# The last K load by partition quarters, a new order of TensorE's work at the end, and another way to the gate and the queries, in a one-token attention kernel

## The chip, the cores and the metric

The kernel runs on one core of a Trainium2 chip. The metric is the device time in microseconds (us). The span in a profile is some 2.1 us shorter than the measured time of the same run (before: 2523.2 against 2525.35). Repeated runs of one kernel lie within about 0.2%, so 5 us. In the lines of profiles below, PE is TensorE, DVE VectorE, ACT ScalarE and SP SyncE, and L324 is line 324 of that kernel.

## The reference

One token attends over a long cache, and a small gate network multiplies the result:

```python
B, Sq, D = 1, 1, 448;  H, Sk, Dh = 16, 65536, 256;  F = 1792
xn = layernorm(x)
q  = (xn @ wq).reshape(B, Sq, H, Dh).transpose(0, 2, 1, 3)
p  = softmax(einsum("bhqd,bhkd->bhqk", q, k_cache) * Dh ** -0.5)
o  = einsum("bhqk,bhkd->bhqd", p, v_cache)
s  = o.transpose(0, 2, 1, 3).reshape(B, Sq, H * Dh) @ wo
g  = silu(silu(xn @ w1) @ w2)
return x + s * g
```

K and V are bf16 and make 1.07 GB of the 1.084 GB that are read. No byte of them is used twice.

## The kernel before

The caches are read in 64 blocks each of 8 MB: 128 keys in each of the 128 partitions (rows) of SBUF, the memory on the chip that loads write to; 64 KB per partition. Three buffers of that size hold K or V in turn. VectorE and ScalarE make the scores of a K block, TensorE multiplies the exponentials with a V block, two keys per product. Semaphores free the buffers for the next load, which SyncE issues. (The code is cut and shortened; the comments are added.)

```python
def load_k(i, s):                      # a block of K over all 128 partitions
    take(sp, vf[s])
    sp.dma_start(out=R[s][:, :], in_=block(Kd, i)).then_inc(kl[s], 16)
...
def load_keys(T, src, k0, k1, s):      # keys k0 to k1 of every partition
    w = slice(k0 * Dh, k1 * Dh)
    sp.dma_start(out=T[:, w], in_=src[:, w]).then_inc(s, 16)
...
        take(sp, vf[0])                # after the loop: the last K, in two halves of 4 MB
        load_keys(R[0], Kl, 0, HK, kl[0])
        load_keys(R[0], Kl, HK, KB, kh[0])
        take(sp, kf[2])                # then V, in pieces
        ...
        # TensorE at the end (shortened)
        keys(psO2, 0, 1, vz, zl, 0, 2, True, od)
        pe_turn()                      # transposes one result row (line 346)
        project(...)                   # products with wo (line 662)
        ...
        keys(psO, 0, 1, vz, zl, 2, 3, True)
        pe_turn()
        keys(psO, 0, 1, vz, zl, 3, len(vz), False, od)
        act_out()
        project(*pieces[2])
        t = pe_turn(tok=True)
        ...
        project(pieces[3][0], H1); project(H1, H)   # last head, then result
```

The head of the kernel computes gate's first product as 112 products of one column each, and the 16 queries as 64 products 256 wide.

## Time and profile before

| | before |
|---|---|
| measured time | 2525.48 us, median of 3 (2525.09 to 2526.38) |
| span of the profile | 2523.2 us |
| bytes read | 1084.29 MB |
| mean rate of the DMA engines | 430 GB/s |
| VectorE busy | 2233.7 us, 89% |
| TensorE busy | 1198.1 us, 47% |

The page's line of GB/s has one figure for each of 40 equal slices, 63 us long:

```profile
GB/s 423 417 430 433 434 431 433 433 432 432 432 432 432 433 434 437 434 435 433 433 433 432 432 432 432 432 433 434 439 434 433 433 433 433 432 432 432 432 412 346
```

After the first slices the rate is flat at some 432, and only the last two, where small pieces of V and the end fall, are clearly lower. One stretch of 20 us in which the last K comes in (length, then busy us of TensorE, its weight loads, VectorE, ScalarE, GpSimd with the count of instructions, TensorE's granted clock, DMA share, GB/s):

```profile
2446.00:2466.00 20.00, 14.24 (x72) 6.28 (x69) 12.14 (x59) 10.45 (x51) 0.00 (x0) 0.90 0.98 418
```

### The profile page before, as it was taken

How to read it: one execution, taken by the hardware profiler on the slowest of the kernel's cores; microseconds unless marked ns; L12 is line 12 of the kernel's file. 1: busy time of each engine (PE TensorE's matmuls, PEld its weight loads, DVE VectorE, ACT ScalarE, POOL GpSimd, SP SyncE). 2: the span in 40 equal slices, each digit the busy share in tenths (PEclk: the TensorE clock that was granted, in tenths of full speed). 3: DMA queues.
4: the chain of work that ended last, by engine and by line, in shares of the span. 5: the costliest groups of instructions: out<-in, count | busy, mean ns of one | idle time of the engine just before them, and what ended most of it. 6: DMA issues, size and time to landing. Idle time of an engine off the chain costs nothing. (4 is left out here: it accounts for less than half of the span.)

```text
span 2523.2 us, 29918 instructions
## 1 busy us (share of the span) xinstructions
PE 1198.1 (47%) x5125; PEld 500.5 (20%) x5125; DVE 2233.7 (89%) x10281; ACT 1443.9 (57%) x6992; POOL 2.5 (0%) x13
## 2 busy tenths in 40 slices
PE   3353543534535435445354354454553543534556
PEld 2121211212212112112121121221221211212222
DVE  6989889889899898898898988988989889889886
ACT  3656556556555565565565655655656556556554
POOL 0000000000000000000000000000000000000000
PEclk7676767767767767677676676676766767767778
DMA  9999999999999999999999999999999999999998
GB/s 423 417 430 433 434 431 433 433 432 432 432 432 432 433 434 437 434 435 433 433 433 432 432 432 432 432 433 434 439 434 433 433 433 433 432 432 432 432 412 346
DMA packets 22728, 1084.52 MB, mean 430 GB/s; under 512 B 2354, under 2 KB 4532, under 8 KB 4916
## 3 DMA queue, kind: packets, MB, share of 16 engines
q1 hardware_dynamic: 22706, 1084.30, 99.5%
q8 instruction: 6, 0.10, 0.0%
q14 instruction: 14, 0.11, 0.0%
q10 hardware_dynamic: 2, 0.00, 0.0%
HBM read 1084.29 MB, written 0.00 MB: 430 GB/s over the span
## 5 line engine op out<-in xcount | busy, mean ns | idle before, releaser
L271 ACT ACTIVATE R<-R 128x256 bf16<-128x256 bf16 x3328 | 1330.7, 401 | 697.1 <-ACTq L154 697.1
L249 DVE CUSTOM_DVE_ANT_0 R<-R,qcur 128x256 bf16<-128x256 bf16 x4864 | 1700.2, 417 | 0.0
L318 PE MATMUL bank<-R,PV 128*2 128x512 bf16 x4096 | 1023.7, 416 | 32.4 <-DMA R<-in_A_v_cache_dram 15.3
L238 DVE TENSOR_TENSOR R<-R,qcur 128x3328 bf16<-128x3328 bf16 x256 | 482.6, 1885 | 198.7 <-DVEq L154 198.6
L271 ACT ACTIVATION_READ_ACCUMULATOR R<-R 128x1 f32 x3328 | 620.2, 186 | 2.6 <-issue 2.6
L330 PE MATMUL bank<-ident,rmax 128*1 128x128 bf16 x65 | 17.1, 263 | 1021.6 <-PEq L154 1021.6
L318 PEld LDWEIGHTS bank<-R,PV 128*2 128x2 bf16 x4096 | 365.0, 90 | 663.1 <-issue 208.0
L249 DVE DVE_READ_ACCUMULATOR2_ANT S<- 128x1 f32 x4864 | 383.5, 79 | 0.0
L346 PE MATMUL bank<-eye,O 2*128 2x1 f32 x536 | 98.0, 300 | 236.8 <-PEq L154 236.8
L330 PEld LDWEIGHTS bank<-ident,rmax 128*1 128x1 bf16 x65 | 5.2, 79 | 1026.1 <-issue 1025.9
L346 PEld LDWEIGHTS bank<-eye,O 2*128 2x128 f32 x536 | 94.2, 257 | 254.8 <-issue 254.8
L284 ACT ACTIVATE hist<-bank 128x1 f32 (+1 forms) x65 | 11.1, 171 | 203.4 <-ACTq L154 203.4
L305 ACT COPY hist<-bank 128x2 f32 (+1 forms) x66 | 10.5, 160 | 120.0 <-ACTq L154 120.0
L214 DVE TENSOR_REDUCE gmax<-bank 1x1 bf16<-1x128 f32 x65 | 18.2, 281 | 36.2 <-DVEq L154 36.2
L231 DVE CAST qcur<-bank 128x256 bf16<-128x256 f32 x64 | 27.2, 425 | 20.2 <-DVEq L154 18.3
L297 ACT COPY O<-bank 2x512 f32<-2x512 f32 x67 | 37.5, 559 | 9.1 <-ACTq L154 9.1
L286 ACT ACTIVATE PV<-S,hist 128x128 bf16<-128x128 f32 (+1 forms) x65 | 26.0, 400 | 13.4 <-ACTq L154 13.1
L358 PE MATMUL bank<-q,ident 16*128 16x256 bf16 x63 | 24.4, 387 | 0.0
L224 DVE COPY S<-S 128x128 f32<-128x128 f32 (+1 forms) x65 | 14.7, 226 | 9.5
L225 DVE TENSOR_REDUCE rmax<-S 128x1 bf16<-128x128 f32 (+1 forms) x65 | 18.2, 279 | 0.0
L336 PE MATMUL bank<-gmax,ones_row 1*128 1x1 bf16 x65 | 10.3, 158 | 15.9 <-PEq L154 15.9
L336 PEld LDWEIGHTS bank<-gmax,ones_row 1*128 1x128 bf16 x65 | 6.5, 99 | 33.3 <-issue 33.3
(65 smaller groups left out, 101.7 us busy)
## 6 DMA issues: line engine op xcount, KB each, us to landing
R<-in_A_k_cache_dram SPq DMA_DIRECT2D x4, 4096.0 KB, 23.4
R<-in_A_v_cache_dram SPq DMA_DIRECT2D x7, 2048.0 KB, 23.1
R<-in_A_wq_dram SPq DMA_DIRECT2D x1, 3072.0 KB, 12.7
R<-in_A_wo_dram SPq DMA_DIRECT2D x2, 1120.0 KB, 17.5
R<-in_B_w_dram SPq DMA_DIRECT2D x1, 1568.0 KB, 27.2
R<-in_B_w_dram SPq DMA_DIRECT2D x1, 1344.0 KB, 5.8
R<-in_A_v_cache_dram SPq DMA_DIRECT2D x1, 1024.0 KB, 15.8
R<-in_A_v_cache_dram SPq DMA_DIRECT2D x2, 512.0 KB, 17.0
```

Of the source, the lines that this page charges most:

```text
L214: dve.reduce_max(out=gmax[0:1, :], in_=ps_m[0:1, :], axis=AX.X).then_inc(gm, 1)
L225: dve.reduce_max(out=rmax[:, :], in_=S[:, c0:c1], axis=AX.X).then_inc(rm, 1)
L231: dve.tensor_copy(out=qcur[:, :], in_=ps_q).then_inc(sd, 1)
L238: m = dve.tensor_tensor(out=pair, in0=pair, in1=qcur[:, None, :].to_broadcast([P, NA, Dh]), op=ALU.mult,)
L249: ins = dve.tensor_tensor_reduce(out=Kv[:, c, :], in0=Kv[:, c, :], in1=qcur[:, :], scale=1.0, scalar=0.0, op0=ALU.mult, op1=ALU.add, accum ...
L271: ins = act.activation(out=prod, in_=prod, func=ACT.Identity, accum_out=S[:, c : c + 1],)
L286: act.activation(out=PV[s][:, c0:c1], in_=S2[:, c0:c1], func=ACT.Exp, bias=col(0, 1), scale=scale, accum_out=col(1, 2),).then_inc(pv, 1)
L297: act.copy(out=O[:, :], in_=po).then_inc(oc, 1)
L318: ins = pe.matmul(po, lhsT=PV[t][:, c : c + 2], rhs=R[s][:, c * Dh : (c + 2) * Dh], start=(start and c == k0), stop=(stop and c == k1 - 2),)
L330: pe.matmul(ps_m[0:1, :], lhsT=rmax[:, 0:1], rhs=ident[:, :], start=True, stop=True).then_inc(tm, 1)
L346: ins = pe.matmul(ps_t[:, a : a + 1], lhsT=Ov[:, j, a, :], rhs=eye2[:, j : j + 1], start=(j == 0), stop=(j == 1),)
L358: pe.matmul(ps_q, lhsT=ident[0:H, at(h)].to_broadcast([H, P]), rhs=q16[:, :], start=True, stop=True,).then_inc(qr, 1)
```

## The change

The change means to cut what lies at the ends of a stream that is full in between. It loads the last K in eight pieces by partition quarters, moves work of TensorE into its pauses while the last V arrives, computes gate's first product as a row (16 wide products) that is then transposed, and makes the queries of two heads in one product.

```diff
-    vz = cuts(0, 32, 64, 96, 112, 120, 128)
+    vz = cuts(0, 32, 64, 80, 96, 112, 120, 128)
-    pieces = cuts(0, 5, 10, 14, 16)
+    pieces = cuts(0, 5, 12, 14, 16)
+    kr = cuts(0, 32, 64, 96, 128)
...
-        load_keys(R[0], Kl, 0, HK, kl[0])
-        load_keys(R[0], Kl, HK, KB, kh[0])
+        for (c0, c1), sm in zip(cuts(0, HK, KB), (kl[0], kh[0])):
+            for p0, p1 in kr:
+                load_keys(R[0][p0:p1, :], Kl[p0:p1, :], c0, c1, sm)
...
-        for f in range(FC):               # gate: 112 products of one column
-            for z in range(2): ...
+        for g, b in enumerate((0, 1, 5, 6)):   # gate: 16 products of 1x448
+            ...
+            t = mark("act", act.copy(out=h1r[:, g * FQ : (g + 1) * FQ], in_=bank[b][0:1, 0:FQ]))
         for f in range(FC):
+            ins = pe.matmul(ps_h[:, f : f + 1], lhsT=h1r...[:, f, :], rhs=ones_sq[0:1, 0:1], ...)
...
-        for h in range(H):                # 64 products, 256 wide
+        for j in range(HP):               # 32 products, 512 wide
...
-        keys(psO2, 0, 1, vz, zl, 0, 2, True, od)
+        keys(psO2, 0, 1, vz, zl, 0, 1, True)
         pe_turn()
+        keys(psO2, 0, 1, vz, zl, 1, 2, False, od)
...
         project(h0 + 3, h1)
-        act_softmax(LAST + 1, 0, HK, KB)
+        pe_turn()
...
-        keys(psO, 0, 1, vz, zl, 2, 3, True)
-        pe_turn()
-        keys(psO, 0, 1, vz, zl, 3, len(vz), False, od)
+        keys(psO, 0, 1, vz, zl, 2, len(vz), True, od)
```

(Cut: the tiles and offsets that follow from these, VectorE's wait, which now counts all loads of a half, and where ScalarE's parts of the end are written down. Some comments are added and some lines shortened.)

More of the change, by code (lines that the diff above doesn't have):

```diff
@@ L60 @@
     NHA = H * 2
+    HP = H // 2
     scale = float(Dh) ** -0.5
@@ L74 @@
     qcur = pool.tile([P, Dh], bf16, name="qcur")
-    q16 = pool.tile([H, Dh], bf16, name="q16")
+    q8 = pool.tile([HP, 2 * Dh], bf16, name="q8")
     S = pool.tile([P, KB], fp32, name="S")
@@ L109 @@
     wq_t, n = rest(0, DF * HD + HD // 2)
-    Z, n = rest(n, DX * H * H)
+    Z, n = rest(n, DX * HP * HP)
     w1_t, n = rest(n, DF * F + F // 2)
@@ L114 @@
     xz, n = rest(n, 2 * P)
+    h1r, n = rest(n, 2 * F)
     assert n <= KW
+    h1r = h1r[0:1, :].bitcast(fp32)
     xn, xz = xn[0:1, :], xz[0:1, :].rearrange("o (z n) -> o z n", z=2)
@@ L127 @@
     ps_q, ps_y, ps_ao, ps_tot = bank[4][:, 0:Dh], bank[5][0:1, 0:D], bank[6][0:1, 0:D], bank[7]
-    psO2, ps_qh = bank[4][0:2, :], bank[3][0:H, 0:Dh]
+    psO2, ps_qh = bank[4][0:2, :], bank[3][0:HP, :]
     ps_xt, ps_h = bank[2][:, 0:DX], bank[7][:, 0:FC]
@@ L232, in dve_block @@
         halves = between is not None
-        take(dve, kl[s], 16)
+        n = 16 * len(kr) if halves else 16
+        take(dve, kl[s], n)
         for k in range(NSTEP):
             if k == NSTEP // 2:
-                take(dve, kh[s], 16)
+                take(dve, kh[s], n)
             pair = Kv[:, k * SUB + ND : (k + 1) * SUB, :]
@@ L356, in pe_query @@
     def pe_query(i):
-        h = i // NB
+        j = i // (2 * NB)
+        o = ((i // NB) % 2) * Dh
         pe.matmul(
             ps_q,
-            lhsT=ident[0:H, at(h)].to_broadcast([H, P]),
-            rhs=q16[:, :],
+            lhsT=ident[0:HP, at(j)].to_broadcast([HP, P]),
+            rhs=q8[:, o : o + Dh] if isinstance(o, int) else q8[:, bass.ds(o, Dh)],
             start=True,
@@ L489 @@
         for c in range(DX):
-            w = Z[:, c * H * H : (c + 1) * H * H]
+            w = Z[:, c * HP * HP : (c + 1) * HP * HP]
             t7 = mark("dve", dve.tensor_copy(
-                out=w[:, 0 : (H - 1) * (H + 1) + 1 : H + 1],
-                in_=xnT[:, c : c + 1].to_broadcast([P, H]),
+                out=w[:, 0 : (HP - 1) * (HP + 1) + 1 : HP + 1],
+                in_=xnT[:, c : c + 1].to_broadcast([P, HP]),
             ))
@@ L505 @@
         pe.wait_ge(dl["w1"], 32)
-        for f in range(FC):
-            for z in range(2):
-                h0 = z * (P // 2)
-                for r, (w, c) in enumerate(rows(w1_t, F, z * (F // 2), (z + 1) * (F // 2))):
-                    ins = pe.matmul(
-                        ps_h[h0 : h0 + P // 2, f : f + 1],
-                        lhsT=w.rearrange("p (q f) -> p f q", f=FC)[:, f, :],
-                        rhs=xnT[:, c : c + 1],
-                        start=(r == 0),
-                        stop=(r == DF),
-                    )
+        FQ = F // 4
+        for g, b in enumerate((0, 1, 5, 6)):
+            for r, (w, c) in enumerate(rows(w1_t, F, g * FQ, (g + 1) * FQ)):
+                ins = pe.matmul(
+                    bank[b][0:1, 0:FQ],
+                    lhsT=xnT[:, c : c + 1],
+                    rhs=w,
+                    start=(r == 0),
+                    stop=(r == DF),
+                )
+            t = mark("pe", ins)
+            need("act", t)
+            t = mark("act", act.copy(out=h1r[:, g * FQ : (g + 1) * FQ], in_=bank[b][0:1, 0:FQ]))
+        need("pe", t)
+        for f in range(FC):
+            ins = pe.matmul(
+                ps_h[:, f : f + 1],
+                lhsT=h1r.rearrange("o (p f) -> o f p", f=FC)[:, f, :],
+                rhs=ones_sq[0:1, 0:1],
+                start=True,
+                stop=True,
+            )
         t = mark("pe", ins)
@@ L543 @@
         ins.then_inc(qr, 1)
-        for h in range(H):
-            for r, (w, c) in enumerate(rows(wq_t, HD, h * Dh, (h + 1) * Dh)):
+        for j in range(HP):
+            for r, (w, c) in enumerate(rows(wq_t, HD, j * 2 * Dh, (j + 1) * 2 * Dh)):
                 ins = pe.matmul(
                     ps_qh,
-                    lhsT=Z[:, (c * H + h) * H : (c * H + h + 1) * H],
+                    lhsT=Z[:, (c * HP + j) * HP : (c * HP + j + 1) * HP],
                     rhs=w,
-                    start=(h == 0 and r == 0),
-                    stop=(h == H - 1 and r == DF),
+                    start=(j == 0 and r == 0),
+                    stop=(j == HP - 1 and r == DF),
                 )
@@ L554 @@
         need("act", t8)
-        t9 = mark("act", act.copy(out=q16[:, :], in_=ps_qh))
+        t9 = mark("act", act.copy(out=q8[:, :], in_=ps_qh))
         pe.wait_ge(dl["w2"], 16)
@@ L694 @@
         act_softmax(LAST, 0, 0, HK)
+        act_out()
         act_sums(0, 2)
-        act_out()
+        act_row(LAST - 1)
         act_sums(0, 3)
-        act_row(LAST - 1)
         take(pe, pv)
-        keys(psO2, 0, 1, vz, zl, 0, 2, True, od)
+        keys(psO2, 0, 1, vz, zl, 0, 1, True)
         pe_turn()
+        keys(psO2, 0, 1, vz, zl, 1, 2, False, od)
+        act_out(psO2)
+        act_softmax(LAST + 1, 0, HK, KB)
         need("pe", t_o)
@@ L717 @@
         weights(N1, NENT, H1, H, (ps_m[:, 0:NL], t15))
-        act_out(psO2)
-        keys(psO, 0, 1, vz, zl, 2, 3, True)
-        pe_turn()
+        t_r = mark("act", act_row(LAST))
         t_g = silu(g_t, ps_y, g_e, t_y)
-        t = mark("act", act_row(LAST))
-        need("dve", t)
+        need("dve", t_r)
         outputs(N1, NENT - 1, H1, H, NL - 1)
-        keys(psO, 0, 1, vz, zl, 3, len(vz), False, od)
+        keys(psO, 0, 1, vz, zl, 2, len(vz), True, od)
         act_out()
```

## The prediction

> **What bounds the kernel now.** I read the page first, then the chain that ended last, then the timelines of TensorE, VectorE and the DMA queue near the end, then busy time by stretches. On the page, lines of its head, slices and queues:
>
> ```profile
> span 2523.2 us, 29918 instructions
> ...
> DVE  6989889889899898898898988988989889889886
> ...
> DMA  9999999999999999999999999999999999999998
> ...
> HBM read 1084.29 MB, written 0.00 MB: 430 GB/s over the span
> ```
>
> The 16 DMA engines are full in every slice; VectorE, the busiest engine, never is. A full stretch moves some 432 GB/s, so the 1084 MB take 1084.3 / 0.432 = 2510 us. The other 13 us are a start, a few holes and what follows the last bytes. The change moves no byte more or fewer, so it can only win or lose in those 13 us, or by the rate of the stream. The chain of work that ended last (start us, us, what):
>
> ```profile
> 2484.34 23.09 DMA R<-in_A_v_cache_dram
> 2507.43 0.04 issue
> 2507.47 3.61 PE bank L318 x16
> 2511.08 1.03 PE bank L346 x8
> 2512.11 3.54 PE bank L318 x16
> 2515.66 1.51 PE bank L662 x8
> 2517.17 1.03 PE bank L346 x8
> 2518.20 0.95 PE bank L662 x4
> ```
>
> A piece of the last V (32 of 128 keys) lands at 2507.43, then TensorE works almost unbroken, then VectorE twice 0.6 us and the write of the result; the span ends at 2523.2. (The measured 2525.5 is 2.3 us over the span.) One more place matters, in TensorE's timeline and in the stretches of 4 us (busy us per engine, clock, DMA share, GB/s):
>
> ```profile
> 2420.18 1.44 PE L318 MATMUL bank<-R,PV 128*2 128x512 bf16 x3
> 2427.17 15.35 PE L318 MATMUL bank<-R,PV 128*2 128x512 bf16 x61 [5.55 <-issue]
> 2442.35 0.17 PE L368 MATMUL bank<-ident 128*1 128x1 bf16 x1
> ```
>
> ```profile
> 2436.00:2440.00 4.00, 4.00 (x21) 1.53 (x19) 4.00 (x25) 3.14 (x16) 0.00 (x0) 1.00 1.14 492
> 2440.00:2444.00 4.00, 3.17 (x19) 1.58 (x17) 4.00 (x14) 0.57 (x1) 0.00 (x0) 1.00 0.46 139
> ```
>
> TensorE stops 5.55 us for "issue", in the middle of a block's products, soon after it left its loop. The buffer for the last K is therefore free only at 2442.5, the queue issues that K at 2442.65, and the DMA engines have run dry: 139 GB/s, a hole of about 2.5 us. VectorE stops likewise on leaving its loop:
>
> ```profile
> 2458.56 0.28 DVE L214 TENSOR_REDUCE gmax<-bank 1x1 bf16<-1x128 f32 x1 [0.94 <-DVEq L154]
> 2465.61 0.42 DVE L231 CAST qcur<-bank 128x256 bf16<-128x256 f32 x1 [6.77 <-DVEq L154]
> ```
>
> Its query was ready at 2458.6 (TensorE's product of line 358 ran at 2458.34) and the first half of the last K had landed at 2454.7 (issued 2442.65, 12.0 us), so this is no wait for data.
>
> [...] The kernel before loads caches only over 128 partitions, at 432 GB/s[...]. [...] stretches with TensorE idle show 0.50, and its 128x512 products come every 0.43 us then, 0.22 us otherwise.
>
> **The change, part by part.**
>
> Gate's first product. Removed: 112 products (6.71 us at 7.45 to 14.16). Added: 16 products of 1x448, which I put at 0.2 to 0.3 us from the 0.2 us pitch of line 662 and 0.32 of line 561, so 3.2 to 5 us; four ScalarE copies of one row, some 0.55 us each from its 1x448 exponential of 0.53, three beside the products; 14 float32 transposes of two passes, 28 x 0.13 us (line 346: eight passes in 1.07) = 3.7 us. It ends near 16 to 17 us instead of 14.2. TensorE then waits for wq, which lands at 17.1, as before. VectorE enters its loop 2 to 3 us later and pays its entry pause there (before: idle 5.74 us up to 20.80), so has its query at 23 to 24; its first work on K started at 27.25, when that half landed. Hidden: 0 us.
>
> Queries of two heads. 64 products (8.79 us) become 32 twice as wide, some 7 us. The result is wanted by the second block, at 61.7 us, and w2's product waits for its DMA till 30.9. Hidden: 0 us. In the loop each query gains a register instruction; TensorE is idle about half the time: 0 us.
>
> TensorE's order at the end. One transpose (1.03 us, line 346) moves before the second V piece, into a 2.37 us wait for it; the transpose of the second half moves before the last products, so the chain holds one transpose instead of two. Four projection products, 4 x 0.2 us, move from after V to before it, with their 448 KB. From before's times: the maximum is broadcast at 2504.95, then 8 projections 1.6 = 2506.65, transpose 1.03 = 2507.7, sums 0.36 = 2508.05. The exponential, done at 2505.98, is in time, and the first V piece, now half as long, too. All 32 products in one go: 32 x 0.222 = 7.1, ending 2515.15 (before 2515.58). Their last piece lands later by 448 KB at the 390 GB/s of these stretches, 1.15 us: 2512.6 becomes 2513.75, plus four products 0.9 = 2514.65, just in time. Copy of the result 0.57 and its semaphores 0.2: transpose at 2515.95 instead of 2517.17. The rest stays. Sum: **-1.2 us**.
>
> Last K by quarters. Two loads of 4 MB become eight of 1 MB over 32 partitions. VectorE waits for all four, so nothing starts earlier; eight issues of some 0.35 us end before the next load may be issued (2457.5). So no gain in order, only a question of rate: see the first rival. If the rate stays: 0 us. Sum of the change without rivals: 2525.5 - 1.2 = 2524.3.
>
> **Rivals.**
>
> (a) [...] VectorE would still have its halves in time[...], but V behind them would land that much later, and the chain has only 0.5 us of room there. It makes 2533 to 2541. [...] Against it: the kernel is tuned, and someone kept this. I give it 4 in 10.
>
> (b) The pause moves. Before its loop TensorE now has some 200 instructions fewer (112+64 products become 30+32, two instructions each, four for float32)[...]. If into the next block, the last K is issued 5 us earlier and the hole of 2.5 us in the stream closes; but the maximum of the block after, and with it VectorE's last block, may be 1 to 4 us later, and that chain (VectorE's end 2503.3, maximum, exponential 2505.98, products) now binds. It makes -2 to +3: 2522 to 2527.
>
> (c) Nothing at the end: the larger second wo load delays V as much as the work saved. 2525.5.
>
> **Range and chances.** Without (a), 6 in 10: 2522 to 2527, middle 2524.3. With it, 4 in 10: 2533 to 2541. I predict the middle of the two together, 2526, with 2521 to 2540 as range. Two per cent is 50 us; no rival reaches it. Faster 0.01, same 0.98, slower 0.01.
>
> **What would show it.** Right: one transpose after the last V products; the last products of V without a gap; the first query and first K times unchanged (27.2 us); wq's product still waiting for its DMA. (a): stretches after the last K's issue at 200 to 300 GB/s instead of 430. (b): the 5.55 us "issue" row gone from the block before, or in another, and the 139 GB/s stretch gone. Wrong: any change of the loop's 38.7 us per pair of loads (59 pairs from the K issue at 116.30 to that at 2398.40), or a head that delays VectorE's first block.

What is cut, at the marks, is what no trace or run of this case had shown. Rival (a) is that a load over 32 partitions runs at about half the rate of one over 128, which no run had shown by then. Its terms came to up to +19 us, and with an overlap of the loads taken off to +9 to +17, which on the 2524.3 without it makes the 2533 to 2541; the 200 to 300 GB/s named at the end rest on the same unshown rate. The 0.50 is TensorE's granted clock, as at 2404 to 2416 us of the profile before.

## The result, and the profile after

The changed kernel takes 2544.6 us, median of 6 runs (2543.09 to 2545.42). The kernel before took 2525.47 in the same rounds (6 runs, 2525.04 to 2528.47). The ratio is 1.0073, 95% interval 1.006 to 1.0086. Ratios here and below are the mean time of one kernel's fast runs over that of the other's of the same rounds, so they are not quite the ratio of the medians. The change costs 19.1 us. That is 0.8%, clear of the noise, and above the predicted range.

The page of the changed kernel, lines of its head, slices and queues:

```profile
span 2542.4 us, 29789 instructions
...
GB/s 420 413 431 429 440 433 430 430 440 433 429 434 439 430 429 441 433 429 431 439 433 429 436 437 430 429 441 433 429 432 440 431 429 439 435 429 429 441 287 338
...
HBM read 1084.29 MB, written 0.00 MB: 426 GB/s over the span
```

The bytes are the same. Up to the last two, the slices hold some 430 GB/s as before; the last but one falls to 287 (before 412). The DMA engines' share is still at nine tenths there: they are busy, and slow. The stretches of the prediction again, and the 20 us of the last K:

```profile
2436.00:2440.00 4.00, 4.00 (x20) 1.54 (x19) 4.00 (x23) 3.27 (x17) 0.00 (x0) 1.00 1.14 492
2440.00:2444.00 4.00, 3.17 (x17) 1.27 (x15) 4.00 (x16) 0.57 (x1) 0.00 (x0) 1.00 0.08 33
```

```profile
2446.00:2466.00 20.00, 14.73 (x74) 6.46 (x72) 11.89 (x60) 10.94 (x54) 0.00 (x0) 0.92 1.01 211
```

211 instead of 418 GB/s at the same DMA share of 1. In the trace's records of single transfers, a 32 KB row of the last K takes 2.55 us where it took 1.21 before; sixteen are under way in both. The second half of the last K lands at 2486.7 us, before at 2465.9.

TensorE at the place of the old pause (start us, us, engine line operation, tiles, shapes, count, idle time before and what ended it):

```profile
2420.35 1.01 PE L324 MATMUL bank<-R,PV 128*2 128x512 bf16 x2
2427.06 15.95 PE L324 MATMUL bank<-R,PV 128*2 128x512 bf16 x62 [5.70 <-issue]
```

The pause is still there, in the same block, 5.70 us long. VectorE's pause at the end of its loop has grown from 6.77 to 9.59 us (in the experiments below it is 9.3 to 10.4 us in e2, e5, e7, e13, e14 and e15, where the last K is as slow, and 6.1 to 7.4 in e3, e4, e6, e12, e16 and e17; why was not tested):

```profile
2468.93 0.42 DVE L236 CAST qcur<-bank 128x256 bf16<-128x256 f32 x1 [9.59 <-DVEq L157]
```

TensorE's end, and the chain that ended last:

```profile
2528.42 7.07 PE L324 MATMUL bank<-R,PV 128*2 128x512 bf16 x32
2535.34 0.92 PE L681 MATMUL bank<-R,OT 128*1 128x448 bf16 x4
```

```profile
2536.32 1.07 PE bank L352 x8
2537.39 0.96 PE bank L681 x4
2538.38 0.62 DVE R L763
2539.02 0.61 DVE x_f L765
```

The last products of V run in one go, and one transpose follows them. The trace has the last bytes of V landing at 2534.2 (before 2512.6), 1.3 us before these products end.

The head, first before and then after (TensorE's gate products and queries, and VectorE's first work on K):

```profile
7.45 6.71 PE L510 MATMUL bank<-xnT,R 128*64 128x1 bf16 x112 [0.91 <-DMA R<-in_B_w_dram]
18.10 8.79 PE L546 MATMUL bank<-R 128*16 128x256 bf16 x64
27.25 1.89 DVE L238 TENSOR_TENSOR R<-R,qcur 128x3328 bf16<-128x3328 bf16 x1 [6.03 <-DVEq L154]
```

```profile
13.44 6.97 PE L529 MATMUL bank<-ones_sq,R 1*128 1x1 f32 x28 [0.61 <-ACT R L526]
21.30 9.16 PE L565 MATMUL bank<-R 128*8 128x512 bf16 x32
28.40 1.89 DVE L244 TENSOR_TENSOR R<-R,qcur 128x3328 bf16<-128x3328 bf16 x1
```

Gate's 16 products take 5.38 us, its 28 transposing passes 6.97, so together nearly twice the old 6.71. The wide queries are not shorter. VectorE begins 1.15 us later.

### The profile page after: what moved, and what is told of

The parts are those of the page before. It is cut to its first block, busy times and chain, and to the rows that moved or that the text cites. A ratio compares the mean times of both kernels' runs of the same rounds, so it can differ in the third digit from the quotient of the medians.

```text
span 2542.4 us, 29789 instructions
## 1 busy us (share of the span) xinstructions
PE 1206.2 (47%) x5025; PEld 497.7 (20%) x5025; DVE 2233.6 (88%) x10281; ACT 1445.9 (57%) x6996; POOL 1.7 (0%) x13
## 2 busy tenths in 40 slices
DMA packets 22968, 1084.52 MB, mean 427 GB/s; under 512 B 2466, under 2 KB 4644, under 8 KB 5028
## 5 line engine op out<-in xcount | busy, mean ns | idle before, releaser
L365 PE MATMUL bank<-q,ident 8*128 (+1 forms) x63 | 24.3, 386 | 7.2 <-issue 0.6
## 6 DMA issues: line engine op xcount, KB each, us to landing
R<-in_A_v_cache_dram SPq DMA_DIRECT2D x3, 1024.0 KB, 15.2
```

The lines of the kernel that those rows point to most:

```text
L365: pe.matmul(ps_q, lhsT=ident[0:HP, at(j)].to_broadcast([HP, P]), rhs=q8[:, o : o + Dh] if isinstance(o, int) else q8[:, bass.ds(o, Dh)], s ...
```

## The experiments

Seventeen kernels ran. They all build on the kernel before, except the first. The theory, P in the expectations, was rival (a) of the prediction: the quarters run at half rate because of the partitions that they write, and this alone costs the time. Rivals were the number and size of the loads, the memory rows that they read, the number of rows per load, and the other parts of the change. The table has what decides: the rate in the stretch from 2446 to 2466 us, the span, and the measured time. (Where the last K is issued earlier, as in e1 and e6, the last 2 us of the stretch are V already.) In the cuts of the edits, VectorE's wait for as many loads as there are is left out.

| run | GB/s, 2446 to 2466 us | span us | median us (before, same rounds) | ratio (95%) |
|---|---|---|---|---|
| e1 change without quarters | 419 | 2525.4 | 2527.30 (2527.02) | 0.9998 (0.9984 to 1.0011) |
| e2 quarters only | 209 | 2543.6 | 2546.74 (2527.02) | 1.0079 (1.0063 to 1.0094) |
| e3 eight pieces by keys | 428 | 2523.0 | 2525.21 (2527.02) | 0.9994 (0.9979 to 1.0009) |
| e4 partitions 32 to 95 in one load | 313 | 2536.1 | 2538.17 (2527.02) | 1.0041 (1.0026 to 1.0057) |
| e5 every second row of 32 to 95 | 226 | 2544.0 | 2545.42 (2528.07) | 1.0072 (1.0042 to 1.0101) |
| e6 every fourth row | 419 | 2524.9 | 2527.05 (2528.07) | 0.9999 (0.9970 to 1.0028) |
| e7 quarters in order 0, 2, 1, 3 | 209 | 2544.0 | 2546.27 (2528.07) | 1.0075 (1.0046 to 1.0104) |
| e8 end only | 421 | 2522.3 | 2524.93 (2525.66) | 0.9992 (0.9979 to 1.0006) |
| e9 gate row only | 413 | 2523.5 | 2525.71 (2525.66) | 0.9997 (0.9982 to 1.0012) |
| e10 pauses hidden | 419 | 2527.6 | 2529.54 (2525.66) | 1.0010 (0.9996 to 1.0024) |
| e11 end, and pauses hidden | 416 | 2525.6 | 2527.56 (2525.66) | 1.0005 (0.9991 to 1.0019) |
| e12 every fourth row written, quarters read | 414 | 2524.4 | 2525.49 (2526.32) | 0.9995 (0.9966 to 1.0024) |
| e13 quarters written, every fourth row read | 211 | 2543.2 | 2545.38 (2526.32) | 1.0074 (1.0044 to 1.0103) |
| e14 halves 0 to 63, 64 to 127 | 211 | 2543.7 | 2545.03 (2526.32) | 1.0072 (1.0043 to 1.0102) |
| e15 every eighth row | 211 | 2542.9 | 2545.65 (2525.55) | 1.0078 (1.0049 to 1.0108) |
| e16 every second row of all | 417 | 2524.8 | 2529.14 (2526.32) | 1.0009 (0.9980 to 1.0038) |
| e17 every fourth row of 32 to 95 | 285 | 2537.0 | 2539.35 (2525.55) | 1.0053 (1.0024 to 1.0083) |

### Is it the quarters, and is it their number?

**e1_whole_rows** is the changed kernel with the last K over all partitions:

```diff
-    kr = cuts(0, 32, 64, 96, 128)
+    kr = cuts(0, 128)
```

> The changed kernel with the last K loaded again in two loads over all 128 partitions; all else as changed. Theory P ([...]this alone costs the 19 us): the stretches after that load's issue go back from 215 to 430 GB/s and the time is the kernel before's, less 1.2 us of the tail, plus some 0.5 us that the later start of VectorE's first block costs: 2524.0 to 2525.5. Rival T (TensorE's new order at the end, or the larger second wo load, costs part of it): over 2528.

The whole loss is gone; everything else in the change together is worth nothing that can be told from zero. (The median is above the expected 2525.5, but so was the kernel before in these rounds, with 2527.02. The gain of some 0.7 us that the expectation had was not seen.) **e2_quarters_only** is the reverse, the loop with `kr` alone put into the kernel before:

> The kernel before with nothing changed but the last K in eight loads, four partition quarters of each half. Theory P: 215 GB/s for some 40 us after the issue at about 2443, and 2543 to 2547. Rival T: under 2535.

It loses 19.7 us between the medians, and its stretch is that of the changed kernel:

```profile
2446.00:2466.00 20.00, 14.65 (x74) 6.45 (x71) 11.59 (x58) 10.86 (x53) 0.00 (x0) 0.92 1.01 209
```

So the quarters alone cost the time. **e3_key_pieces** loads the last K in as many pieces of as many bytes, but each over all partitions, 16 keys wide:

```diff
+    kr = cuts(0, 16, 32, 48, 64)
...
+        for c, sm in ((0, kl[0]), (HK, kh[0])):
+            for k0, k1 in kr:
+                load_keys(R[0], Kl, c + k0, c + k1, sm)
```

> The kernel before with the last K also in eight loads of 1 MB, but each of 16 keys over all 128 partitions: as many loads, as many bytes in each, as many issues. Theory P[...]: about 430 GB/s and the time of before, 2524 to 2527. Rival S (eight small loads cost it, by their number, their size or their issue): 2540 or more.

No loss. Eight issues and loads of 1 MB are not the cause.

### Which partitions are slow?

From here on only the rows of each load change. **e4_middle_rows** takes partitions 32 to 95 in one load and the two outer quarters after it:

```diff
+    kr = ((32, 96), (0, 32), (96, 128))
```

> The kernel before with each half of the last K in three loads: partitions 32 to 95, then 0 to 31, then 96 to 127. [...] Theory P: 4.2 MB at 430 and 4.2 MB at 215 GB/s, 9.8 + 19.5 = 29.3 us instead of 19.5, so +10 us: 2534 to 2537, with stretches of 400 GB/s and more between those of 215. Rival N (fewer than 128 partitions[...] is what costs it, whichever they are): 64 partitions as slow as 32, 2542 to 2547.

Somewhat over half of the loss is left (11.2 of 19.7 us, a little above what was expected). So the middle rows come fast, though they are only 64, and the outer quarters slowly. In the transfer records most rows of the middle loads take 1.21 us, as before, and those of the outer quarters 2.3 to 2.6. A stretch in which the middle of the second half comes:

```profile
2462.00:2466.00 4.00, 0.59 (x6) 0.51 (x5) 0.01 (x1) 0.00 (x0) 0.00 (x0) 0.58 1.21 387
```

**e5_every_second_row**, **e6_every_fourth_row** and **e7_alternate_quarters** came next:

```diff
+    kr = (slice(32, 96, 2), slice(33, 96, 2), slice(0, 32), slice(96, 128))        # e5
+    kr = (slice(0, 128, 4), slice(1, 128, 4), slice(2, 128, 4), slice(3, 128, 4))  # e6
+    kr = ((0, 32), (64, 96), (32, 64), (96, 128))                                  # e7
```

> The kernel before with each half of the last K in four loads of 32 rows, 1 MB each, like the quarters, but the first two take every second partition of 32 to 95[...]; then partitions 0 to 31 and 96 to 127. Theory P[...]: half of the bytes at 430 and half at 215 GB/s, about +10 us, as with partitions 32 to 95 in one load. Rival N (32 rows[...] make a load slow, whichever they are): all at 215 GB/s, +19 us, 2544 or more.

> The kernel before with each half of the last K in four loads of every fourth partition. [...] If it counts [...]: 430 GB/s, 2525 to 2528. If it counts [...]: 215 to 250 GB/s, over 2540. Between the two[...].

> The kernel before with the quarters in the order 0, 2, 1, 3[...]. My prediction's term [...] would make this clearly faster than the order 0, 1, 2, 3: under 2540. [...] as slow, 2544 to 2548.

e6 runs at full rate:

```profile
2446.00:2466.00 20.00, 16.10 (x75) 6.74 (x72) 12.96 (x66) 9.15 (x44) 0.00 (x0) 0.93 0.98 419
```

So 32 rows in a load are not slow in themselves. e7 shows that another order of the quarters gains nothing, so the overlap of them that the prediction took off was not there: 209 GB/s, as with the quarters in order. But e5 contradicts the theory as it stood. Its first two loads take the same partitions 32 to 95 that came at 387 GB/s in e4, and still it loses about as much as the quarters (17.4 us between the medians; e7 loses 18.2). Something in the theory was wrong, and the next runs asked what.

### The partitions written, or the memory rows read?

**e12_spread_rows_from_quarters** and **e13_quarters_from_spread_rows** separate the two. The last K then stands in the wrong partitions, on purpose; the comparison with the reference still passed, presumably as one block of 64 moves the result too little.

```diff
+    kr = tuple(zip([slice(r, P, 4) for r in range(4)], [slice(32 * r, 32 * r + 32) for r in range(4)]))  # e12
+    kr = tuple(zip([slice(32 * r, 32 * r + 32) for r in range(4)], [slice(r, P, 4) for r in range(4)]))  # e13
...
+            for d, p in kr:
+                load_keys(R[0][d, :], Kl[p, :], c0, c1, sm)
```

> The last K's loads write every fourth partition (which ran at full rate) but read 32 neighbouring rows of memory (as in the slow quarters); the last block's result is wrong on purpose. If the partitions written decide the rate: no loss, 2525 to 2529 us, span near 2524, and the 4-us stretches from 2448 to 2464 at 380 to 450 GB/s. If the memory rows read decide it: half rate, 2542 to 2548 us, span near 2543, those stretches at 150 to 260 GB/s.

> The reverse: the loads write quarters of 32 neighbouring partitions and read every fourth row of memory; wrong on purpose in the last block. If the partitions written decide: half rate, 2542 to 2548 us, span near 2543. If the memory rows decide: no loss, 2525 to 2529 us.

Stretches of e12, then of e13, in the columns as above:

```profile
2446.00:2466.00 20.00, 15.12 (x76) 6.62 (x73) 12.19 (x60) 11.32 (x56) 0.00 (x0) 0.93 0.97 414
```

```profile
2446.00:2466.00 20.00, 17.71 (x78) 7.38 (x78) 13.44 (x68) 9.63 (x47) 0.00 (x0) 0.89 1.00 211
```

The partitions written decide (every fourth 414 GB/s, quarters 211), and the memory rows read do not.

### How many rows, and in which order?

**e14_halves** uses loads of 64 rows, 0 to 63 and 64 to 127 (`kr = cuts(0, 64, 128)`). **e16_halves_by_second_row** uses loads of 64 rows too, every second one over all 128 partitions (`kr = (slice(0, P, 2), slice(1, P, 2))`).

> Loads of partitions 0 to 63 and 64 to 127, twice as many rows per load as a quarter and as many as the middle loads that ran at full rate in the run with partitions 32 to 95. [...] half rate for all 8 MB, 2542 to 2548 us, span near 2543. If the 32 rows of a load[...] were what is slow: no loss, 2525 to 2529 us.

> Loads of every second partition, 64 rows each, over all 128: [...]it differs from the slow run with every second row of 32 to 95 only in its span and count. [...] no loss, 2525 to 2529 us. [...] half rate, 2542 to 2548 us[...].

e14 is as slow as the quarters (211 GB/s), so 64 rows in a load are not enough to make it fast. e16 runs at full rate (417 GB/s). (One of its two runs was 4.6 us longer than the other; the profile is of the shorter one and has no loss.)

**e17_middle_by_fourth_row** goes back to the partitions of e5. Where e5 has two loads of 32 rows, it has four of 16. **e15_every_eighth_row** also has 16 rows per load, spread over all 128 partitions.

```diff
+    kr = [slice(r, 96, 4) for r in range(32, 36)] + [slice(0, 32), slice(96, P)]  # e17
+    kr = [slice(r, P, 8) for r in range(8)]                                       # e15
```

> The same partitions 32 to 95 that were slow in loads of every second row, now in four loads of every fourth row: 16 rows[...]. Quarters 0 to 31 and 96 to 127 follow as before. [...] the middle at full rate, only the outer quarters slow, +10 to +11 us as with partitions 32 to 95 in one load, 2536 to 2538 us. If strided loads of 32 to 95 are slow whatever their order: +19, 2544 to 2546 us.

> Eight loads per half, each of every eighth row over all 128 partitions: 16 rows[...]. [...] half rate, +19 us, 2542 to 2548 us. If a load only has to span all partitions: no loss, 2525 to 2529 us.

Two stretches of e17, the second time that the middle rows come and the outer quarters behind them:

```profile
2462.00:2466.00 4.00, 0.00 (x0) 0.00 (x0) 0.00 (x0) 0.00 (x0) 0.00 (x0) 0.50 1.13 387
2468.00:2476.00 8.00, 0.00 (x0) 0.00 (x0) 8.00 (x40) 3.60 (x17) 0.00 (x0) 0.50 0.88 190
```

The first of them in e5, where the same partitions are on their way in loads of every second row:

```profile
2462.00:2466.00 4.00, 0.10 (x1) 0.02 (x1) 0.00 (x0) 0.00 (x0) 0.00 (x0) 0.59 0.96 215
```

The same partitions come at 387 GB/s in loads of 16 rows, every fourth, and at 215 in loads of 32, every second. In the transfer records, a row of e17's middle loads takes 1.22 us and one of its outer quarters some 2.4; in e5 nearly all take 2.3 to 2.6. So it is not only which partitions are written that counts, but also how they are divided among loads. e17's total is 13.8 us over before where 10 to 11 were expected; the sign and the place are as expected. In the profiles e17 and e4 lie close: from issue to landing the last K takes 36.7 and 35.9 us, against 23.2 before and 43.6 in e2, so that both save less than the expected 10 us. That remainder I leave open. e15 is slow (211 GB/s): to span all partitions is not enough.

What makes one division fast and another slow was not shown. The number of rows alone doesn't: loads of 16 were fast in e17's middle and slow in e15, loads of 32 fast in e6 (419 GB/s) and slow in e5, loads of 64 fast in e16 and slow in e14. Which rows were under way at one moment is not in the trace.

### The other parts

**e8_end_only** is the kernel before with the change's order at the end (`vz`, `pieces`, and TensorE's and ScalarE's last part).

> The kernel before with the change's order at the end alone (V pieces, wo pieces, transposes). My step says -1.2 us: 2.2 us from the end of the last V products to the last transpose's end instead of 2.6, and the last V products 0.4 us earlier, in a run whose pauses fall as in the profile before. Measured ratio 0.9990 to 1.0000. If the end only trades a transpose for a later V: ratio 1.000 and the last V products later by 1 us.

Its TensorE near the end:

```profile
2508.30 7.07 PE L318 MATMUL bank<-R,PV 128*2 128x512 bf16 x32
2516.21 1.07 PE L346 MATMUL bank<-eye,O 2*128 2x1 f32 x8
```

The last transpose begins at 2516.21, in this view of the profile before at 2517.10, and the span is 0.9 us shorter. The medians differ by 0.7 us, but the interval includes 1, so the gain is seen in the trace and not settled in the times. Its median is the lowest of all versions, but not clear of before. **e9_gate_row_only** is the kernel before with the change's gate code:

> The kernel before with the gate's first product as one row alone. My prediction said hidden: first block of VectorE still at 27.2 us. The profile of the changed kernel says its 28 transposing passes took 6.97 us, not 3.7, and VectorE's first block began at 28.4. So I expect the gate's products to end near 20.4 instead of 14.2, VectorE's entry pause to end near 27, and its first block at 27.3 to 28.5; time 0 to +1 us.

VectorE's first work on K begins at 27.91 instead of 27.25 us, and the end does not move.

The prediction spoke of the hole of 2.5 us before the last K and of the pauses that cause it. **e10_pauses_hidden** tries to take them away: VectorE and ScalarE leave their loops three blocks earlier, and TensorE gets 24 products without use before each of its last two blocks, so that its pause falls on them. (What the pauses are was not shown; the first case of the expectation is that they move with this.) **e11_end_and_pauses** adds e8's end, and TensorE's product of the maxima one V piece earlier.

```diff
-        pe_block(NBLK - 3, 0)
         pe_turn()
+        pe_fill(24)
+        pe_max(NBLK - 3)
+        pe_v(0)
+        pe_turn()
+        pe_fill(24)
         pe_v(1)
```

> The kernel before with the pauses at the loops' ends moved: VectorE and ScalarE leave their loops three blocks earlier, where each block has some 4 us of slack, and TensorE has 24 filler products before it waits for the maximum of the block after its loop, and 24 before the next block's products. [...] TensorE's 5.6 us gone from the block's products, the last K issued near 2437 instead of 2442.6, the 139 GB/s stretch gone, VectorE's last block begun near 2459 instead of 2466; the end then hangs on V's landing, 2.5 us earlier: about -2.5 us. If the pauses are something else (a wait on data, the clock): no change of the time.

> The change's order at the end, and the pauses moved as in the run before, and the maximum of the last block's first half taken one V piece earlier. The end then hangs on V's landing alone, with one transpose after it: about -4 us, 2521 where the kernel before takes 2525. If the order at the end is worth nothing where V's landing decides: no better than with the pauses moved alone.

Both were misses: e10 came out 4 us slower than before where 2.5 us less were expected, and e11 2 us below e10, which is e8's part. In e10, the stretches at the old hole, and the same 20 us later:

```profile
2440.00:2444.00 4.00, 0.00 (x0) 0.00 (x0) 4.00 (x25) 3.95 (x19) 0.00 (x0) 0.78 0.86 371
2460.00:2464.00 4.00, 4.00 (x20) 1.56 (x19) 1.82 (x12) 0.24 (x2) 0.00 (x0) 1.00 0.88 356
```

The hole is filled (371 instead of 139 GB/s), as the last K is issued at 2440.08 instead of 2442.65. But TensorE's filling products (6.93 us) stand in front of the next block of V, and VectorE waits for TensorE:

```profile
2466.83 0.28 DVE L214 TENSOR_REDUCE gmax<-bank 1x1 bf16<-1x128 f32 x1 [4.86 <-DVEq L154]
```

The next V loads are issued at 2461.86 instead of 2457.51, VectorE's last block starts 1.4 us later, and the end comes 4.4 us later. What the hole gave was taken back later. e1 says the same in another way: there TensorE had no pause in this block at all, in the same TensorE program in which the changed kernel's profile has one.

```profile
2420.30 15.95 PE L324 MATMUL bank<-R,PV 128*2 128x512 bf16 x64
```

Its last K was issued at 2436.39, 6.3 us earlier than before, and its span was no shorter (2525.4). e6 has the TensorE program of the kernel before, and no pause in this block either (nor have e13 and e14). Its profile shows where the gain goes. Its last K was issued at 2436.43, and the piece of V that bound the end before landed at 2505.06 instead of 2507.43, so the stream did gain what the hole had cost. But VectorE's last block began at 2467.50 instead of 2466.07, the last maximum was broadcast at 2506.37 instead of 2504.95, and the last products of V, which now waited for no load, began at 2508.59 instead of 2507.47. In e6 VectorE's last block bound the end; in e10 the piece of V did, landing at 2510.07.

## Why the prediction was wrong

**The bound: right.** The bytes and the DMA share did not change, and the time moved by the rate of the stream alone, in one place.

**The quarters: the step that failed.** The prediction took an overlap of the quarters off the full loss of its rival (a), came to +9 to +17 us and gave the rival 4 in 10. That they come at half the rate was right; the size and the weight were off. Its own first sum, up to +19, was the answer: 8.39 MB at the 211 GB/s of the stretch take 39.8 us, at the 418 of before 20.1; the difference is 19.7 us, and e2 lost 19.7. The overlap that I took off was an estimate without a measurement under it, and it was not there: the stretch runs at 209 GB/s with the quarters in order (e2) and in another order (e7). The weight of 6 in 10 against rested on "the kernel is tuned, and someone kept this", which is no reading of a trace. The range was also worked out wrongly: with these weights the middle of the two cases is 0.6 x 2524.3 + 0.4 x 2537 = 2529.4, not 2526, and its upper end, 2540, left out the sum's own +19, which makes 2543.3. The measured time is 2544.6.

**K in time for VectorE: right in effect, with luck.** VectorE goes through the first half of its last block without a gap (2468.93 to 2486.22) and the second half has landed at 2486.7, before it is wanted at 2491. But the first half landed at 2466.71, which is 0.6 us after VectorE had begun with it in the profile before (2466.07); the longer pause (9.59 us) hid that. The loss came by V behind it, as written: TensorE then waits 29.17 us for the first piece of the last V but one.

**The end: right in its times, its worth not settled.** -1.2 us was predicted, 0.9 measured in e8's profile, and the interval of the times includes no gain. The products ended at 2515.37 (2508.30 + 7.07) where 2515.15 was worked out (before they ended at 2515.66, not at 2515.58 as I had read), the transpose began at 2516.21 instead of 2515.95. "Just in time" held in the changed kernel, where V's last bytes land 1.3 us before the products end, with the last four products, 0.9 us, still to come. In the sum, 20.4 us (spans of e2 and before) less 1.2 (spans of e2 and the changed kernel) is the 19.2 between the spans of the changed kernel and before; these are single profiles, and the spans of one kernel differ by some 2 us.

**The head: sizes wrong, effect right.** Gate's transposing passes took 0.25 us each (6.97 / 28), not the 0.13 that I took from line 346, a row of another shape. So gate's products ended at 20.4 us, wq's product did not wait for its DMA, though the prediction had it wait, and VectorE had its query at 27.94 us and not at 23 to 24. The wide queries took 9.16 us instead of 7, and the stretches of the changed kernel say why:

```profile
17.00:20.00 3.00, 3.00 (x13) 3.00 (x14) 0.00 (x0) 0.00 (x0) 0.00 (x0) 0.50 0.96 415
21.30:25.30 4.00, 4.00 (x11) 1.27 (x11) 0.02 (x1) 0.00 (x0) 0.00 (x0) 0.50 0.90 388
26.00:29.00 3.00, 3.00 (x15) 1.21 (x14) 1.02 (x2) 0.00 (x0) 0.00 (x0) 1.00 1.19 503
```

The first row is transposing passes, the other two are query products. The granted clock is 0.50 from 15.3 us, in the passes, until some 25.6 us, though TensorE is busy; 11 query products take 4.0 us there, and 15 take 3.0 us at full clock. Before, the clock was 1.00 in all of this. At 0.2 us each the 32 would have taken 6.4 us. e9, which has the passes and the old queries, shows the same half clock from about 15.2 to 25.4 us, so it comes with the gate row. Why was not shown: the passes had only 0.61 us of idle time ahead of them. "Hidden" it was not quite, as VectorE's first block was 1.15 us late. It cost nothing that can be seen: the last V load of the loop is issued at 2419.01, before at 2418.84, and e9's ratio is 0.9997.

**Rival (b): did not come in the changed kernel, but its chain is real.** TensorE has fewer instructions ahead of its loop, and yet its pause stayed in the same block, 5.70 us long (before 5.55), after two products instead of three. With the same TensorE program the pause was absent in e1, and with that of the kernel before in e6, e13 and e14. So the place of an instruction alone does not decide whether it comes. Where it was absent, e1 and e6 went as the rival had it: the last K some 6 us earlier, VectorE's last block 1.4 to 1.8 us later, that chain binding, and a time that can't be told from before (ratios 0.9998 and 0.9999). Closing the hole isn't worth its 2.5 us.

**Rival (c)** did not occur: e8's transposes came earlier, in spite of the larger second load of wo.

## What to carry to other kernels

When a kernel lives on a full DMA stream, a load over a part of the partitions can be a slower load and not only a smaller one, depending on which part: here the same bytes took twice the time in quarters, or in the halves 0 to 63 and 64 to 127 (209 to 211 GB/s against 418), and lost nothing when cut by keys (428), or in every fourth or second partition of all 128 (419 and 417). If a load must be cut, cut it along the bytes of a partition (here the keys), so that each load covers all partitions. And when two cases of a prediction lie far apart, settle which one holds from the pages and the trace before taking a middle.
